# Opening of a two-layer attention and MLP kernel: resident bias, reordered row maxima, transposes moved to TensorE, held weight loads

## The chip, the cores and the metric

The kernel runs on one core of a Trainium2 chip. The metric is the device time of one execution in microseconds (us). The core's engines run their own instruction streams in order: TensorE (PE; its weight loads are listed apart as PEld), VectorE (DVE), ScalarE (ACT), GpSimd (POOL) and SyncE (SP), which here only issues transfers. ACT issues transfers too, on a queue of its own. An engine waits for another by semaphores.

## The reference

Two layers, each of windowed attention and a squared-ReLU MLP, over 2048 rows of width 640, in float32. Attention has 32 heads of width 20; each row sees itself and the 255 rows before it.

```python
def _A_ref(x, wqkv, wo):
    H = 32; Dh = D // H; W = 256
    qkv = (x @ wqkv).reshape(B, S, 3, H, Dh) ...
    scores = jnp.einsum("bhqd,bhkd->bhqk", q, k) * (Dh ** -0.5)
    mask = (idx[:, None] - idx[None, :] >= 0) & (idx[:, None] - idx[None, :] < W)
    p = _softmax(jnp.where(mask, scores, -1e9), axis=-1)
    return einsum("bhqk,bhkd->bhqd", p, v) ... @ wo

def _B_ref(x, w1, b1, w2, b2):
    h = jnp.maximum(x @ w1 + b1, 0)
    return (h * h) @ w2 + b2

x = x + _A_ref(_layernorm(x), wqkv, wo)
x = x + _B_ref(_layernorm(x), w1, b1, w2, b2)     # both lines twice
```

## The kernel before

**Units.** The rows of a layer are cut into 8 units of 256 rows; with two layers there are 16 units, u = 0 to 15. Every dense product is made of float16 pieces: an operand is split into a high and a low half, and three matmuls (high·high, high·low, low·high) per 128-deep slice are summed by `mm3` (L334), whose matmuls all carry L339. A matmul has 256 or 320 columns. Its accumulators, and the outputs of transposes (`tr`) and of p·v (`pv`), take turns in two PSUM tiles (`mm_tile`, L240, bufs=2): the third one waits until the first has been evicted. Evicting is mostly a pair: ACT writes the high half, then DVE the low half (L534 and L537 for queries and keys, L389 and L390 for transposed rows).

**Stages of a unit.** Layernorm (DVE, with one power on POOL); transposed rows `yT`; queries and keys (`stage_qk`), which are written to device memory, read back in another layout by head ("spread", L589) into `qt` and `kt`; values (`stage_v`); then 8 quads of 4 heads. A quad runs twice through the scores: first for the row maxima (`max_quad`: TensorE writes two PSUM blocks `bb`, DVE reduces them), then, with the maxima folded into the operands (`max_out` L783, a small transfer `qt<-mT` of L757), for the exponentials (`exp_quad`: TensorE, ACT L825, masks on POOL and DVE) and p·v (`pv_quad`, L931). Both passes use the same `bb`, so a pass waits until the engine that reads the one before it is done. After the last quad the unit's outputs, written to device memory (L951), come back (`load_o`, L969: transfers L984, L985), are divided by the row sums (L1017, L1020), split into halves (L1024, L1027) and multiplied by `wo` (`stage_o`), normalised, transposed by TensorE (`stage_y` for the opening, L403) or by transfers (`y_cross`), and go through the MLP (`stage_f`, with weights `w_s` and the intermediate `hh`).

**Order.** All five queues are written in an order that the program decides while it is built. Operations are posted as jobs with an engine, a cost, dependencies and a priority (`post`, L144); `pump` (L161) puts the jobs that can start by the planner's clock, and that clock decides how many dense matmuls go between two quads. `urgency` (L332, and L1381 from u = 1 on) holds priorities. In the opening (`ahead_all`, L1350, and `flow`, L1301) the quads of unit 0 are mixed with the dense work of units 0, 1 and 2; unit 0 has no rows before it, so its quads are smaller (L735, L886). The rows of unit 1 and 2 are transposed by transfers there (`ln_early`, L467, in which ACT L452 and DVE L456 make the two halves and SP transposes them, L459).

**Weights.** They are loaded in float32 and converted by ACT (L271) and DVE (L272) while the opening runs; `bulk` (L153) posts the loads of `wo`, `w1` and `w2` on ACT's queue when the planner takes the transfers to be idle. b2 is loaded and broadcast to all partitions in every unit (`add_b2`, L1066), into one of the two `xt` buffers that layernorm uses too; POOL adds it to the residual.

**An eviction's dependency.** In `evict` (L540), `left[k]` holds which unit last used the staging buffer, and the transfers that have read it. The comparison at L543 sets a tuple of two against a tuple of one, so it is always unequal, and every chunk is planned after the transfer of the chunk before it.

Of the kernel before, what the change touches and what calls it, by code (L numbers as in the profile page):

```python
# [10 lines left out]
F32 = mybir.dt.float32  # L11
# [5 lines left out]
P = 128  # L17
# [28 lines left out]
def kernel(ctx: ExitStack, tc: tile.TileContext, x, wqkv, wo, w1, b1, w2, b2, out):  # L46
# [35 lines left out]
    for h in range(2):  # L82
        nc.gpsimd.tensor_copy(drop[h * Q:(h + 1) * Q], edges[h * Q:(h + 1) * Q, :, h * Q:(h + 1) * Q])
    b1s = sb.tile([P, FC], F32, name="b1s")
    kts = []
    for i in range(3):
# [31 lines left out]
    TAIL = {"A": 115.0, "D": 85.0, "G": 40.0, "S": 0.0}  # L118

    class Job:  # L120
        def __init__(self, eng, cost, fn, deps, nb, prio, size=0, idle=False, land=LAND):
# [4 lines left out]
        def ready(self):  # L126
            return all(d.end is not None for d in self.deps)

        def start(self):
            t = max([clk[self.eng], self.nb] + [d.end + LAT for d in self.deps])  # L130
            return max(t, moved[0] - 2200.0) if self.idle else t

# [198 lines left out]

    urgency = {"out": 0, "od": 1, "cross": 1, "mask": 0, "turn": 1, "exp": 1, "ln": 1, "y": 0.5, "clear": 0.5}  # L332

# [168 lines left out]
    def stage_qk(u, which=(0, 1)):  # L502
# [9 lines left out]
        for j, c0 in order:  # L512
# [27 lines left out]
            def evict(wait, k=k, n=n, c0=c0, high=high, low=low, jobs=jobs, j=j, dst=dst, qd=qd):  # L540
                pr = urgency["out"]
                old = left.get(k, ())
                if k and (j, u) != old[:1]:  # L543
                    old = left[k] = ((j, u), [], old[1] if old else [])
                hi_ = post("A", 60 + 212 * n, high, *(old[2] if k else ()), wait=wait, prio=pr)
                lo_ = post("D", 70 + 267 * n, low, hi_, prio=pr)
                jobs.append(lo_)
                if u == 0:
                    wrote = leave(u, j, dst, qd, lo_, c0, n)
                elif c0 + n == KC:  # L550
                    wrote = leave(u, j, dst, qd, lo_, 0, KC)
                else:
                    return
                if k:
                    old[1].append(wrote)
# [17 lines left out]
    def leave(u, j, dst, qd, ready, c0, n):  # L573
# [17 lines left out]

        wrote = dma(write, n * P * 3 * T * 2, ready, n=2, prio=0)

# [15 lines left out]
    def stage_v(u, which=range(4)):  # L609
        yT = yTs[u]  # L610
        for i in range(2):
            if u == 2:
                yield Want(sums[i], bank=False)
            vt = vts[(2 * u + i) % 6][0]
            for h in range(2):
# [51 lines left out]
    def max_quad(n, later=False):  # L667
# [62 lines left out]
        else:  # L730
# [7 lines left out]
            apart[0] = True  # L738
            for w in range(4):
                j, i = divmod(w, 2)  # L740
                for e in range(2):
                    to = bb[e][:, w % 3, w // 3 * T:w // 3 * T + (1 + i) * P]
                    if i:
                        reduce(e, w, to, maskw, 2 * P)
                    else:
                        reduce(e, w, to, maskw[:, P:], P)
            mxjobs[u, G] = list(bbjobs)

# [220 lines left out]
    def load_o(u, late=False, free_=()):  # L969
# [16 lines left out]

        loaded = dma(load, P * (KC + 1) * T * 4, *wrote, *free_, n=2, prio=0)
        if u == NU - 1:
            both = sb.tile([P, 2, D], F32, name="x1", tag="qt", bufs=2)
            x1 = [both[:, i] for i in range(2)]  # L990
        elif u == NU - 2:

            x1 = [krow[(u - 1) % 3][:, i * D:(i + 1) * D] for i in range(2)]
        else:
            x1 = [sb.tile([P, D], F32, name="x1", bufs=2) for i in range(2)]
# [70 lines left out]
    def add_b2(u):  # L1066

        b2s = sb.tile([P, D], F32, name="xt", tag="xt", bufs=2)
        load = dma(lambda: nc.sync.dma_start(b2s, bass.AP(tensor=b2.tensor, offset=b2.offset, ap=[[0, P], [1, D]])),
                   P * D * 4)  # L1070
        js = []
        for i in range(2):
            for h in range(2):
                hs = slice(h * HD, (h + 1) * HD)
                js.append(post("G", 827, lambda x1=x1s[u, i], hs=hs:
                               nc.gpsimd.tensor_tensor(x1[:, hs], x1[:, hs], b2s[:, hs], op=ALU.add), load, prio=2))
        return js
# [223 lines left out]
    def flow(todo, dense):  # L1301
# [3 lines left out]
        while todo:  # L1305
# [15 lines left out]
            if kind == "m":  # L1321
                max_quad(n)
            elif kind == "r":
                max_out(u, G)
            elif kind == "s":
                quad = exp_quad(n)
            else:
                pv_quad(n, quad)
            pump()
# [20 lines left out]
    def ahead_all():  # L1350
        yield from stage_qk(0)
        ln_early(1, place)
        yield from stage_v(0, range(2))
        ln_load(2)
        yield from stage_v(0, range(2, 4))
# [12 lines left out]
    load_o(0)  # L1368
    dma(lambda: nc.sync.dma_start(b1s, b1.rearrange("(c p) -> p c", p=P)), 8192, *ols[0][2], prio=2)

    while not all(j.end is not None and j.end <= now[0] + LOOK for j in bbjobs):
        c = next(rest)
        if not isinstance(c, Want):
            used[0] += c
            step(c)
    left_over = 3 * (QKC + VC) - used[0]
    rate[0] = 320.0
    for u in range(1, NU):
        last = u == NU - 1
        if u == 1:  # L1380
            urgency.update({"out": 0, "od": 1.5, "cross": 1, "mask": 0, "turn": 0.7, "exp": 0.7, "ln": 0.5, "y": 1, "clear": 0.5})  # L1381
# [47 lines left out]
```

## Time and profile before

| | |
|---|---|
| time, median of 3 (lowest, highest) | 1560.52 us (1558.01, 1563.2) |
| the profiled execution: time, span | 1561.46 us, 1559.6 us |
| mean granted TensorE clock | 0.997 of full speed |
| PE idle in the whole span | 26.1 us |
| transfers | 162.16 MB, mean 104 GB/s |

The span runs from the first to the last instruction; 1.9 us lie around it. In rows of the timeline the first number is the start in us, the second the duration; then engine, line, operation, what it writes and reads, count, and in brackets the idle time before it and what ended it. [...]

### The profile page before, as it was taken

The page shows a single profiled execution, that of the slowest core. Times are in us where ns is not written, and L with a number is a line of the kernel's source. Part 1 is how long each engine was busy: PE and PEld are TensorE (multiplying, and loading weights), DVE is VectorE, ACT ScalarE, POOL GpSimd, SP SyncE. Part 2 cuts the span into 40 slices and gives each one's busy share as a digit, 9 for nine tenths or more (in the row PEclk, how much of TensorE's full clock was granted, in tenths as well). Part 3 has the DMA queues.
Part 4 walks back from the last instruction along what each step waited for, and adds up shares of the span by engine and source line. Part 5 has one row for each costly group of instructions (what it writes and reads, how often), then busy time and mean ns, then how long its engine had stood idle before and what let it go on. Part 6 is the DMA issues. An engine that isn't in the chain of part 4 may idle for free. (4 is left out here: it accounts for less than half of the span.)

```text
span 1559.6 us, 58897 instructions
## 1 busy us (share of the span) xinstructions
PE 1533.5 (98%) x25822; PEld 1198.6 (77%) x25822; DVE 1043.3 (67%) x2244; ACT 669.7 (43%) x1365; POOL 451.8 (29%) x847
## 2 busy tenths in 40 slices
PE   8998999999999999999999999999999999999999
PEld 6666778787787877878777787877878777786777
DVE  8878775666757667675666757667675676667642
ACT  4565435334453443435343453444435335354422
POOL 1223314232141331413224141321413214142412
PEclk9999999999999999999999999999999999999999
DMA  9975354352534424344462434425243342542120
GB/s 271 209 201 127 80 121 92 106 114 54 123 88 114 105 74 126 69 126 89 99 130 63 119 91 119 100 70 132 67 126 89 94 117 65 122 90 59 30 68 18
DMA packets 248745, 162.16 MB, mean 104 GB/s; under 512 B 96552, under 2 KB 232232, under 8 KB 248488
## 3 DMA queue, kind: packets, MB, share of 16 engines
q1 hardware_dynamic: 242120, 148.89, 38.7%
q10 hardware_dynamic: 6368, 9.50, 2.1%
q8 instruction: 202, 3.31, 0.9%
q14 instruction: 55, 0.45, 0.1%
HBM read 84.68 MB, written 52.95 MB: 88 GB/s over the span
## 5 line engine op out<-in xcount | busy, mean ns | idle before, releaser
L825 ACT ACTIVATE pt<-bb 128x640 f32<-128x640 f32 (+2 forms) x512 | 311.9, 684 | 167.6 <-PE bb L840 148.9
L854 POOL TENSOR_SCALAR_AFFINE_SELECT pt<-pt 64x256 f32<-64x256 f32 x448 | 199.3, 445 | 582.1 <-ACT pt L825 560.0
L339 PE MATMUL acc<-y,w_s 128*128 128x256 f16 x2880 | 330.2, 274 | 1.2 <-DVE y L390 1.2
L339 PE MATMUL acc<-w_s,hh 128*128 128x320 f16 (+1 forms) x2340 | 326.7, 297 | 0.1
L339 PEld LDWEIGHTS <-w_s 128*128 128x128 f16 x2880 | 276.4, 98 | 40.9 <-issue 2.0
L339 PEld LDWEIGHTS <-hh 128*128 128x128 f16 x2340 | 222.1, 98 | 86.8 <-issue 0.4
L720 DVE TENSOR_REDUCE mx<-bb 128x4 f32<-128x1024 f32 x224 | 273.2, 1224 | 6.8
L339 PE MATMUL acc<-yT,wq_s 128*128 128x256 f16 x2250 | 259.1, 273 | 3.0 <-DVE qd L537 1.2
L339 PEld LDWEIGHTS <-wq_s 128*128 128x128 f16 x2400 | 229.6, 98 | 37.3 <-issue 4.3
L863 DVE COPY_PREDICATED_SCALAR pt<-drop,zero 128x256 f32 x224 | 99.9, 497 | 134.3 <-ACT pt L825 133.8
L1130 DVE TENSOR_TENSOR hh<-r,hh 128x256 f16<-128x256 f32 x192 | 98.3, 525 | 110.8 <-ACT hh L1127 105.7
L931 PE MATMUL pv<-pt,vt 64*32 64x192 f32 (+5 forms) x3840 | 166.7, 302 | 0.9 <-DVE y L390 0.6
L943 ACT COPY ot<-pv 128x256 f32<-128x256 f32 x128 | 47.6, 372 | 276.1 <-PE bb L931 247.2
L1124 POOL TENSOR_TENSOR r<-r 128x256 f32<-128x256 f32 x192 | 121.9, 655 | 127.9 <-ACT r L1120 125.3
L931 PE MATMUL bb<-pt,vt 64*32 64x128 f32 (+3 forms) x3584 | 153.5, 301 | 0.0
L717 DVE COPY_PREDICATED bb<-maskq,bb 128x256 f32<-128x256 uint16 x224 | 93.8, 423 | 85.7 <-PE bb L703 80.0
L931 PEld LDWEIGHTS pv<-pt,vt 64*32 64x32 f32 (+1 forms) x3840 | 125.5, 106 | 31.7 <-issue 3.7
L339 PE MATMUL acc<-wo_s,od 128*128 128x320 f16 x960 | 139.6, 299 | 2.2 <-ACT od L1024 2.0
L339 PE MATMUL acc<-wq_s,yT 128*128 128x320 f16 x900 | 132.1, 302 | 5.0 <-DVE qd L537 4.2
L1120 ACT ACTIVATE r<-acc,b1s 128x256 f32<-128x256 f32 x192 | 81.1, 476 | 98.6 <-PE acc L339 96.5
L339 PEld LDWEIGHTS <-od 128*128 128x128 f16 x960 | 90.9, 98 | 40.6 <-ACT od L1024 2.3
L339 PEld LDWEIGHTS <-yT 128*128 128x128 f16 x900 | 87.1, 98 | 40.0 <-issue 6.2
(103 smaller groups left out, 1476.3 us busy)
## 6 DMA issues: line engine op xcount, KB each, us to landing
qt<-qk SPq DMA_DIRECT2D x30, 480.0 KB
kt<-qk SPq DMA_DIRECT2D x30, 480.0 KB
o<-ot SPq DMA_DIRECT2D x256, 42.0 KB
qk<-qd SPq DMA_DIRECT2D x15, 640.0 KB
od<-o SPq DMA_DIRECT2D x14, 640.0 KB
qk<-yl SPq DMA_DIRECT2D x13, 640.0 KB
xt<-in_A_x_dram SPq DMA_DIRECT2D x16, 320.0 KB
x<-in_A_x_dram SPq DMA_DIRECT2D x16, 320.0 KB
```

Of the source, the lines that this page charges most:

```text
L339: nc.tensor.matmul(acc, lhs(a, c), rhs(b, c), start=(k == 0), stop=(k == 3 * nk - 1))
L717: nc.vector.copy_predicated(wins[:, :, 4 * Q:], later, wins[:, :, :Q])
L720: nc.vector.tensor_reduce(most, wins[:, :, Q:], axis=mybir.AxisListType.X, op=ALU.max)
L825: return lambda: nc.scalar.activation(room_of(box)[:, a:b], bank[:, a:b], AF.Exp, scale=SCALE / (QS * QS))
L854: nc.gpsimd.affine_select(out=m, in_=m, pattern=[[0, 4], [-1 if k else 1, Q]], base=0, fill=0.0, compare_op=ALU.is_gt if k else ALU.is_ge, ...
L863: nc.vector.copy_predicated(m, drop[:, k:k + 1, :].bitcast(mybir.dt.uint16).to_broadcast([P, 4, Q]), zero.unsqueeze(1).to_broadcast([P, 4, ...
L931: nc.tensor.matmul(pv[h][32 * jj:32 * (jj + 1), q0 * Q:(q0 + w) * Q], vf[r, c:c + 32], boxes[e]["pt"][r, a:b], start=(k == 0), stop=(k == ...
L943: nc.scalar.copy(ot[:, qd % 2], to)
L1120: nc.scalar.activation(box["r"], acc[:, f, :], AF.Relu, bias=b1s[:, f0 + f:f0 + f + 1], scale=1.0 / (YS * WS))
L1124: nc.gpsimd.tensor_tensor(box["r"], box["r"], box["r"], op=ALU.mult)
L1130: nc.vector.tensor_sub(hh[:, 1, f, :], box["r"], hh[:, 0, f, :])
```

## The change

- b2 is loaded once into a tile of its own, `b2s`, after unit 0's output has been requested; the additions on POOL wait for no load of their own any more.
- `max_quad` for the first unit of a layer (units 0 and 8) posts the four reductions of one `bb` block, then the four of the other; for unit 8 the second four may be posted after the p·v of the quad beside it.
- In the opening, unit 1's rows are transposed by TensorE (`ln_t`), after the first half of unit 0's values; unit 2's remain with transfers.
- Bulk loads are held from the last p·v of unit 0 until the read of unit 0's output has been issued, by a marker job in `quiet`; a write of unit 2's queries or keys that is posted in that time waits too.
- The comparison in `evict` is made between like things, priorities of the opening change, and the later priorities set in from unit 3 instead of unit 1.

```diff
+    b2s = sb.tile([P, D], F32, name="b2s")
...
+    quiet = []
...
         def ready(self):
-            return all(d.end is not None for d in self.deps)
+            return all(d.end is not None for d in self.deps) and not (self.idle and any(q.end is None for q in quiet))
...
-            return max(t, moved[0] - 2200.0) if self.idle else t
+            return max([t, moved[0] - 2200.0] + [q.end for q in quiet]) if self.idle else t
...
-    urgency = {"out": 0, "od": 1, "cross": 1, "mask": 0, "turn": 1, "exp": 1, "ln": 1, "y": 0.5, "clear": 0.5}
+    urgency = {"out": 0, "od": 0.5, "cross": 1, "mask": 0, "turn": 1, "exp": 1, "ln": 1, "y": 1, "clear": 0}
...
-                if k and (j, u) != old[:1]:
+                if k and (not old or old[0] != (j, u)):
...
-        wrote = dma(write, n * P * 3 * T * 2, ready, n=2, prio=0)
+        wrote = dma(write, n * P * 3 * T * 2, ready, *(quiet if u == 2 else ()), n=2, prio=0)
...
                 yield Want(sums[i], bank=False)
+                need(sums[i])
...
-            for w in range(4):
-                j, i = divmod(w, 2)
-                for e in range(2):
-                    to = bb[e][:, w % 3, w // 3 * T:w // 3 * T + (1 + i) * P]
...
+            def each(e):
+                for w in range(4):
+                    i = w % 2
+                    reduce(e, w, bb[e][:, w % 3, w // 3 * T:w // 3 * T + (1 + i) * P], maskw[:, (1 - i) * P:], (1 + i) * P)
+                mxjobs[u, G] = list(bbjobs)
+
+            each(0)
+            behind.append(lambda: each(1))
+            if not later:
+                tops()
...
         loaded = dma(load, P * (KC + 1) * T * 4, *wrote, *free_, n=2, prio=0)
+        if u == 0:
+            loaded.gates.append(quiet[0])
...
-        b2s = sb.tile([P, D], F32, name="xt", tag="xt", bufs=2)
-        load = dma(lambda: nc.sync.dma_start(b2s, bass.AP(tensor=b2.tensor, offset=b2.offset, ap=[[0, P], [1, D]])),
-                   P * D * 4)
...
-                               nc.gpsimd.tensor_tensor(x1[:, hs], x1[:, hs], b2s[:, hs], op=ALU.add), load, prio=2))
+                               nc.gpsimd.tensor_tensor(x1[:, hs], x1[:, hs], b2s[:, hs], op=ALU.add), *b2load, prio=2))
...
+                if n == NQ - 1:
+                    quiet.append(Job("S", 0.0, None, [], 0.0, 0))
                 pv_quad(n, quad)
...
         yield from stage_qk(0)
-        ln_early(1, place)
         yield from stage_v(0, range(2))
+        yield from ln_t(1, place)
         ln_load(2)
...
-    left_over = 3 * (QKC + VC) - used[0]
+    left_over = 3 * (QKC + VC) + LNC - used[0]
...
-        if u == 1:
+        if u == 3:
             urgency.update({"out": 0, "od": 1.5, "cross": 1, "mask": 0, "turn": 0.7, "exp": 0.7, "ln": 0.5, "y": 1, "clear": 0.5})
```

The change moves instructions in all queues of the opening. From the end of unit 1's MLP on, the stream of TensorE is the same as before, instruction for instruction. Three places show what moved.

On ACT, at the end of unit 0's queries and keys (`qd` is the staging of queries, `stg` that of keys and, where an `xt` is read, of unit 1's rows; `vt` are values), before:

```order
L271 ACTIVATE wq_s<-kt_96 128x5x128 x3
L534 ACTIVATE qd<-acc 128x2x256
L534 ACTIVATE stg<-acc 128x2x256
L452 CAST stg<-xt 128x640
L300 DMA w_s<-in_A_wo_dram 32x5x640
L452 CAST stg<-xt 128x640
L534 ACTIVATE qd<-acc 128x256
L534 ACTIVATE stg<-acc 128x256
```

The same place of the changed kernel:

```order
L537 ACTIVATE qd<-acc 128x2x256
L274 ACTIVATE wq_s<-kt_97 128x5x128 x3
L537 ACTIVATE stg<-acc 128x2x256
L537 ACTIVATE qd<-acc 128x256
L537 ACTIVATE stg<-acc 128x256
L626 ACTIVATE vt_98<-acc 128x16x20
L303 DMA w_s<-in_A_wo_dram 32x5x640
L626 ACTIVATE vt_98<-acc 128x16x20
L392 CAST kt_97<-tr 128x3x128
L392 CAST kt_97<-tr 128x2x128
```

The last chunk's two evictions now stand right behind the chunk before; the two casts of unit 1's rows are gone, and the evictions of TensorE's transposes (`tr`) follow the values.

On SP, around the read of unit 0's output (`o`; `rs` and `od` are what is read, `qk_1` unit 2's keys, `mT` the maxima), before:

```order
L757 DMA qt<-mT 1x8x128 x4
L951 DMA o_720<-ot 21x2x256 x4
L984 DMA rs<-o_720 128x1x256
L985 DMA od<-o_720 128x5x256
L583 DMA qk_1_1596<-qd 128x5x512
L585 DMA qk_1_1596<-qd 128x5x256
L589 DMA qt<-qk_0_1344 60x16x256 x2
```

And in the changed kernel:

```order
L762 DMA qt<-mT 1x8x128 x4
L586 DMA qk_1_1543<-qd 128x5x512
L588 DMA qk_1_1543<-qd 128x5x256
L956 DMA o_763<-ot 21x2x256 x4
L989 DMA rs<-o_763 128x1x256
L990 DMA od<-o_763 128x5x256
L592 DMA qt<-qk_0_1297 60x16x256 x2
```

The write of unit 2's keys has moved from behind the read to ahead of the last write of `o`.

On DVE, where that output is divided and split (`mx` are maxima, `ot` the sum of two p·v halves, L863 and L868 clear masked weights), before:

```order
L946 TENSOR_TENSOR ot<-bb_143,ot 128x256
L1017 RECIPROCAL rs<-rs 128x64
L1020 TENSOR_TENSOR od<-od,rs 128x5x64
L1017 RECIPROCAL rs<-rs 128x64
L794 TENSOR_SCALAR mT<-tr 16x128
L795 SCALAR_TENSOR_TENSOR mT<-tr,mT 16x128
L1027 TENSOR_TENSOR od<-od 128x5x64
```

And in the changed kernel:

```order
L951 TENSOR_TENSOR ot<-bb_144,ot 128x256
L275 SCALAR_TENSOR_TENSOR w_s<-kt_97,w_s 128x640
L799 TENSOR_SCALAR mT<-tr 16x128
L800 SCALAR_TENSOR_TENSOR mT<-tr,mT 16x128
L1024 RECIPROCAL rs<-rs 128x64 x2
L1027 TENSOR_TENSOR od<-od,rs 128x5x64 x2
L868 COPY_PREDICATED pt<-drop,zero 128x4x64 x2
L1034 TENSOR_TENSOR od<-od 128x5x64 x2
```

The division now stands behind the maxima's rows `mT`, and so behind the second scores pass of unit 1.

More of the change, by code (lines that the diff above doesn't have):

```diff
@@ L738, in max_quad @@
             apart[0] = True
-            for w in range(4):
-                j, i = divmod(w, 2)
-                for e in range(2):
-                    to = bb[e][:, w % 3, w // 3 * T:w // 3 * T + (1 + i) * P]
[L743 to L747, printed above, removed]
+            def each(e):
[7 more added lines that the diff above has]
+                tops()
     mxjobs = {}
@@ L1369 @@
     dma(lambda: nc.sync.dma_start(b1s, b1.rearrange("(c p) -> p c", p=P)), 8192, *ols[0][2], prio=2)
+    b2load = [dma(lambda: nc.sync.dma_start(b2s, bass.AP(tensor=b2.tensor, offset=b2.offset, ap=[[0, P], [1, D]])),
+                  P * D * 4, *ols[0][2], prio=2)]
     while not all(j.end is not None and j.end <= now[0] + LOOK for j in bbjobs):
```

## The prediction

> **What bounds the kernel now.** First the page's head: one engine is busy nearly throughout.
>
> ```profile
> span 1559.6 us, 58897 instructions
> PE 1533.5 (98%) x25822; PEld 1198.6 (77%) x25822; DVE 1043.3 (67%) x2244; ACT 669.7 (43%) x1365; POOL 451.8 (29%) x847
> ```
>
> TensorE is idle for 26.1 us. Next, stretches of 10 us (PE, PEld, DVE, ACT and POOL busy with counts, granted clock, DMA share, GB/s), and stretches of 3.4 us around the two places where the clock falls.
>
> ```profile
> 20.00:30.00 10.00, 8.35 (x76) 7.18 (x74) 9.68 (x19) 3.94 (x7) 1.61 (x2) 1.00 0.83 206
> 30.00:40.00 10.00, 6.94 (x47) 4.09 (x47) 6.20 (x29) 1.72 (x4) 0.41 (x1) 0.83 1.02 211
> 160.00:170.00 10.00, 10.00 (x208) 8.48 (x206) 8.80 (x17) 6.36 (x15) 4.80 (x9) 1.00 0.52 102
> ...
> 30.83:34.24 3.41, 1.18 (x13) 0.67 (x13) 2.21 (x6) 1.28 (x3) 0.00 (x0) 1.00 0.98 172
> 34.25:37.65 3.40, 3.40 (x14) 1.96 (x13) 2.62 (x16) 0.44 (x1) 0.00 (x0) 0.50 0.92 220
> 126.41:129.81 3.40, 2.11 (x16) 1.38 (x14) 3.18 (x7) 0.78 (x2) 0.00 (x0) 1.00 0.44 122
> 136.65:140.05 3.40, 1.36 (x64) 1.16 (x64) 3.33 (x9) 1.73 (x4) 0.55 (x1) 1.00 0.53 184
> 140.06:143.46 3.40, 2.86 (x44) 2.20 (x45) 2.72 (x6) 1.55 (x4) 0.00 (x0) 0.50 0.00 0
> 143.47:146.88 3.41, 3.41 (x17) 2.43 (x16) 3.07 (x6) 2.49 (x4) 1.95 (x1) 0.50 0.16 22
> ```
>
> From 160 us on nothing is to be had; the opening holds the waits. After a stretch with 1.18 or 1.36 us busy of 3.4 the clock is halved for one or two stretches; after 2.11 it is not. TensorE's own waits, from its timeline:
>
> ```profile
> 25.45 3.44 PE L339 MATMUL acc<-yT,wq_s 128*128 128x256 f16 x30 [0.53 <-DVE qd L537]
> 33.06 0.70 PE L339 MATMUL acc<-wq_s,yT 128*128 128x320 f16 x4 [4.18 <-DVE qd L537]
> 47.61 0.27 PE L886 MATMUL bb<-qt,kt 62*128 62x256 f16 x1 [0.36 <-DMA qt<-mT]
> 48.14 0.49 PE L886 MATMUL bb<-qt,kt 62*128 62x256 f16 x7 [0.26 <-DVE bmv L370]
> ...
> 140.24 1.30 PE L403 MATMUL tr<-ident,xt 128*128 128x128 f32 x5 [1.78 <-DVE xt L378]
> 143.53 8.68 PE L339 MATMUL acc<-y,w_s 128*128 128x256 f16 x63
> ```
>
> The largest, 4.18 us, waits for a PSUM tile that DVE empties late.
>
> **Term 1, the late eviction.** ACT's and DVE's timelines:
>
> ```profile
> 27.60 0.73 ACT L452 CAST stg<-xt 128x640 f16<-128x640 f32 x1 [2.05 <-DVE xt L378]
> 31.09 0.72 ACT L452 CAST stg<-xt 128x640 f16<-128x640 f32 x1 [2.76 <-DVE xt L378]
> 31.72 0.38 ACT L534 ACTIVATE qd<-acc 128x256 f16<-128x256 f32 x1
> 32.59 0.42 DVE L537 SCALAR_TENSOR_TENSOR qd<-acc,qd 128x256 f16<-128x256 f32 x1
> ```
>
> The last query chunk's eviction at 31.72 stands behind a cast that waits for unit 1's layernorm. In the new order no cast is there, and the chunk before is evicted ahead of three weight conversions, which also covers the 0.53. Both waits go (4.7 us), and with them the 3.4 us at half clock from 34.25 (1.7). What is late next is the last chunk's DVE half, due by my reading of the queues 0.8 us ahead of TensorE's need. **-6.4 us**; bounds -7 and 0 (DVE, at 9.68 of 10 busy, late again).
>
> **Term 2, ten transposes on TensorE.** The group of ten near the end, and the eviction and reduction rows:
>
> ```profile
> L403 PE MATMUL bb<-ident,xt 128*128 128x128 f32 x10 | 1.4, 273 | 0.0
> L390 DVE TENSOR_TENSOR yT<-bb,yT 128x384 f16<-128x384 f32 (+1 forms) x4 | 1.9, 489 | 1.1 <-ACT yT L389 1.1
> ...
> 34.23 0.30 DVE L683 CUSTOM_DVE_ANT_0 bb<-bb,maskw 128x128 f32<-128x128 f32 x1 [0.90 <-PE bb L735]
> 36.72 0.14 DVE L683 DVE_READ_ACCUMULATOR2_ANT mx<- 128x1 f32 x1
> ```
>
> The transposes cost 1.4 us. Four groups (3, 2, 3, 2) take turns in two PSUM tiles, so the third waits for the first's eviction, and DVE has unit 0's first eight reductions (34.23 to 36.86, 2.6 us) around the four evictions (1.9): 4.6 us with the start, against 0.95 (seven matmuls of 0.136), 1.4 and 0.44 (a scores pass) on TensorE. That leaves **+1.8 us** of wait; bounds 0 and 3.5. The removed casts and transfers of unit 1 ran on engines that TensorE no longer waits for, so they give nothing beyond Term 1; SP gets free earlier.
>
> [...]
>
> **Term 3, first exponentials.** 25 more matmuls (2.7 us) stand between the maxima's transfer and the pass that waited 0.36 and 0.26: **-0.6**; bounds -0.6 and +1.
>
> **Term 4, the rest of unit 0's quads.** The waits view of 40 to 130 us:
>
> ```profile
> PE acc L339 <- DVE qd L537: 0.6, 1, 0.6
> PE acc L339 <- DVE stg L537: 0.6, 1, 0.6
> ```
>
> The new order spaces the quads nearly as before. One of these waits follows a maxima transpose that now has 25 matmuls instead of 5 behind it; I take half: **-0.6**; bounds -1.2 and +1.2. The reordered reductions are the same eight, and one pass reads both blocks alternately, so whichever is last counts: nothing.
>
> **Term 5, from the last p·v of unit 0 to the MLP of unit 0.** The pace of its pieces, from starts in TensorE's timeline:
>
> ```profile
> 104.05 4.54 PE L339 MATMUL acc<-yT,wq_s 128*128 128x256 f16 x40
> 108.52 0.76 PE L840 MATMUL bb<-qt,kt 62*64 62x128 f16 x38
> ...
> 162.89 0.76 PE L703 MATMUL bb<-kt,qt 60*64 60x256 f16 x38
> 164.88 2.90 PE L339 MATMUL acc<-y,w_s 128*128 128x256 f16 x25
> ...
> 1513.75 1.79 PE L339 MATMUL acc<-w_s,hh 128*128 128x320 f16 x12
> 1515.38 0.71 PE L403 MATMUL bb<-ident,xt 128*128 128x128 f32 x5
> ```
>
> A matmul takes 0.112 us (4.47 by 40) or, with 320 columns, 0.136 (1.63 by 12); a maxima pass and its p·v 2.0 (1.99), of which I give the pass 0.7. Unit 0's last p·v ended at 104.05, the MLP's first matmul ran at 143.53: 39.5 us. The stretch held 40 and 120 such matmuls, 7 scores passes, 3 p·v and 12 transposes: 31.1 us of work, 8.4 of waiting and half clock. Now the 40, 4 of the 120, one scores pass and a transpose lie outside it, which leaves 25.2 us. The chain beside them:
>
> ```profile
> 104.60 2.64 SPq L951 DMA_DIRECT2D o<-ot  x4
> 110.26 0.59 SPq L984 DMA_DIRECT2D rs<-o  x1
> 109.38 2.49 ACT L825 ACTIVATE pt<-bb 128x640 f32<-128x640 f32 x4 [0.27 <-issue]
> 113.50 0.42 DVE L717 COPY_PREDICATED bb<-maskq,bb 128x256 f32<-128x256 uint16 x1
> 116.70 0.41 DVE L946 TENSOR_TENSOR ot<-bb,ot 128x256 f32<-128x256 f32 x1
> 121.23 0.49 DVE L1027 TENSOR_TENSOR od<-od 128x320 f16<-128x320 f32 x1 [0.22 <-ACT od L1024]
> ```
>
> Counted from the end of that p·v: 30 matmuls, scores, 23 matmuls, maxima and p·v end at 10.5. Three matmuls are left, but the next scores need both reductions and the sum (113.50 to 117.11, 3.6 us): they start at 12.7, a wait of 1.8. The maxima pass directly behind needs four exponentials (2.5 us): 16.2, a wait of 2.6. The division, now behind `mT`, starts at 14.4, and its first half with masks and splits ends at 18.0 (before 17.7). P·v takes until 18.6, 30 matmuls with `wo` until 22.7. DVE has the second half of the division and split (3.0), the reductions and the sum (3.6) behind 18.0, so the next scores wait until 24.6 (1.9); then 30 matmuls, maxima and p·v end at 31.9. The second tile's transposes wait 1.7 for its layernorm, the MLP 1.4 for their eviction: it starts at 36.4, 11.2 us above its work. Against 8.4: **+2.8 us**; bounds -2 and +5. Holding the bulk loads frees the queue for the write and read of `o` (104.60 to 110.26 before), but the write of unit 2's keys now stands ahead of it, so I count no gain; the chain has cover until 14.4.
>
> **Term 6, the clock there.** Before, 3.4 us at half clock follow 143.53 (1.7 lost). Now 3.1 of some 3.7 us before the MLP are idle, so a fall is as likely as not: 1.4 expected, **-0.3**; bounds -1.7 and +1.7.
>
> **Costed at nothing.** 16 broadcasts of b2 become one, beside a DMA share of 0.52. POOL's four additions of a unit now run together, ahead of the squares:
>
> ```profile
> L1076 POOL TENSOR_TENSOR x<-x,xt 128x320 f32<-128x320 f32 x60 | 56.7, 956 | 92.5 <-DMA xt<-in_B_b_dram 81.1 <-issue 11.3
> ```
>
> 3.8 us, against 3.3 us of matmuls before the first square is due; uncovered, 0.5 a unit, 7.5 in all. Unit 8's deferred reductions lie beside a saturated TensorE; uncovered, a wait of 1.3 us per quad.
>
> **Sum.** -6.4 + 1.4 + 1.8 - 0.6 - 0.6 + 2.8 - 0.3 = -1.9 us. The profiled execution took 1561.46 (its span and 1.9 around it), so 1559.6 in its terms; it lies 0.9 above the median of 1560.52, so **1558.6 us**.
>
> **Rivals.** A difference under 0.3% (4.7 us) can hardly be told from none. (a) **The new waits don't show**: the transposes' evictions fit beside other work, the chain after the last p·v waits as long as before, the clock holds at the MLP. For it: before, these places waited mostly 0.3 to 1.8 us. Against it: dense work does run out there. -6.4 + 1.4 - 0.6 - 0.6 - 1.7 = -7.9, taken from 1560.5: 1552.6. (b) **The clock falls in more places**, ending slower: two half-clock stretches behind the transposes (+3.4), one that the waits of Term 5 don't hide (+1.7), two at the MLP instead of the half chance of one (+2.0): +7.1 on the forecast, 1565.7. It decides where a 3.4 us stretch is idle by more than about 1.3 to 2 us (above); Term 2's wait is just there. [...] (c) **The eviction stays late**, since DVE's conversions and not the cast held it: Term 1 goes, 6.4 on the forecast, 1565.0. Against it: ACT waited 2.76 us for that cast.
>
> **Chances.** Forecast 0.50, (a) 0.33, (b) 0.10, (c) 0.07. Faster by over 0.3%: (a) and a tail of the forecast, 0.36. Slower: (b) and the upper part of (c), 0.13. Within: 0.51. The forecast alone spans 1555 to 1562; leaving out 1 in 10 on each side, the range is 1551.5 to 1565.5.
>
> **What would show it.** Right: the values of unit 0 start near 28 us without a wait and at full clock; TensorE waits 1 to 3 us around the transposes near 33 to 36 us; from unit 0's last p·v to the MLP take 35 to 38 us, with waits at the scores behind three matmuls and the maxima behind them. The half clock appears once near the MLP, or not at all. From 160 us on TensorE stays full, and the two kernels differ by a constant. Wrong: waits for POOL in later units, a half clock near 35 us, or a division of `od` that waits for its transfer.

## The result and the profile after

The changed kernel takes **1569.95 us** (median of 6 runs, 1568.83 to 1571.78), the kernel before 1560.65 beside it (6 runs, 1558.01 to 1563.2): ratio 1.006, 95% interval 1.0048 to 1.0073, 9.3 us slower. Forecast were 1558.6 us and a range up to 1565.5; the time lies outside. The profiled execution took 1570.76 us. The page's head, after:

```profile
span 1569.0 us, 58829 instructions
PE 1537.4 (98%) x25832; PEld 1200.7 (77%) x25832; DVE 1044.9 (67%) x2246; ACT 670.8 (43%) x1367; POOL 444.3 (28%) x847
```

TensorE is idle for 31.6 us, before 26.1, and busy for 3.9 us more. The span is cut below at six points that both kernels have: the first matmul of unit 0's values, its first pass for exponentials, the end of its last p·v, its MLP's first matmul, a dense piece near 270 us and one near 1010 us. Three stretches of before, then five of after (length; busy time of PE, PEld, DVE, ACT and POOL; granted clock; DMA share; GB/s):

```profile
33.06:47.61 14.55, 14.07 (x106) 9.09 (x105) 10.93 (x58) 1.75 (x4) 0.55 (x1) 0.88 0.81 186
47.61:104.05 56.44, 54.21 (x650) 38.78 (x651) 41.68 (x129) 34.53 (x72) 14.60 (x33) 1.00 0.87 218
104.05:143.53 39.48, 34.64 (x634) 25.16 (x632) 35.77 (x71) 20.90 (x41) 7.35 (x14) 0.96 0.63 164
```

```profile
10.60:27.87 17.27, 16.56 (x151) 14.61 (x152) 16.92 (x29) 11.66 (x20) 0.55 (x1) 1.00 0.98 305
27.87:48.33 20.46, 18.32 (x143) 12.72 (x140) 16.83 (x68) 4.22 (x10) 1.09 (x2) 0.92 0.85 211
48.33:109.52 61.19, 55.39 (x671) 40.33 (x670) 49.09 (x141) 36.56 (x76) 15.88 (x33) 1.00 0.75 195
109.52:146.31 36.79, 28.60 (x552) 20.30 (x548) 29.99 (x58) 17.74 (x35) 10.09 (x18) 0.95 0.63 158
146.31:274.58 128.27, 127.64 (x2316) 100.59 (x2316) 86.24 (x170) 59.23 (x120) 38.03 (x74) 0.99 0.38 91
```

The values start 5.2 us earlier (27.87), as forecast, but the last p·v ends 5.5 us later (109.52). The first stretch has lost its waits; in the next three TensorE is idle for 2.1, 5.8 and 8.2 us, before for 0.5, 2.2 and 4.8.

Stretches hold different work in the two kernels, so a length alone misleads. **Loss** is here the length minus the work, and work is the count of pieces by their undisturbed pace between starts: 0.109 us a matmul of 256 columns, 0.1365 with 320, 0.69 and 0.44 a large and a small pass, 1.30 and 0.79 a large and a small p·v, 0.11 a transpose. In the traces 148 matmuls of 256 columns take 16.17 us from 11.70 (after), 91 of 320 take 12.36 from 1499.83 (after), the passes 0.69 from 154.00 (after) and 0.44 from 42.01 (before), the p·v 1.29 from 160.28 and 0.79 from 52.56 (after), five transposes 0.54 from 1522.52 (after). Example: 109.52 to 146.31 is 36.8 us, its pieces make 25.1, the loss is 11.7. Loss holds waits and half clock. A starts at the first dense matmul (10.84 us before, 10.68 after), G ends with the last one; G's 72 matmuls of 160 columns are counted like those of 320, which takes the same 4.9 us off G's loss in every column. All kernels of this table were profiled once; the work is that of before in the first and e2_red, that of after in the others.

| stretch | work before / after | before | after | e1_alt | e2_red | g2_half | g4_alt_steady1 | h1_alt_steady2 |
|---|---|---|---|---|---|---|---|---|
| A, to unit 0's values | 16.4 / 16.4 | 5.9 | 0.8 | 0.8 | 5.9 | 0.8 | 0.8 | 0.8 |
| B, to the first exponentials | 11.8 / 15.6 | 2.8 | 4.8 | 2.7 | 4.8 | 3.6 | 2.7 | 2.7 |
| C, to the last p·v | 48.9 / 51.1 | 7.5 | 10.1 | 6.8 | 10.0 | 8.0 | 8.2 | 7.0 |
| D, to the MLP | 30.8 / 25.1 | 8.7 | 11.7 | 11.6 | 7.9 | 14.4 | 14.0 | 12.2 |
| E, to about 270 us | 120.5 / 121.3 | 4.3 | 6.9 | 8.5 | 2.4 | 6.9 | 2.7 | 7.9 |
| F, to about 1010 us | 726.5 / 726.5 | 15.2 | 16.8 | 15.0 | 19.1 | 15.5 | 14.6 | 15.0 |
| G, to the end | 533.3 / 533.3 | 13.2 | 14.7 | 14.5 | 13.2 | 12.3 | 12.9 | 14.1 |

After against before, from values not yet rounded: -5.0 +2.1 +2.6 +3.0 +2.6 +1.6 +1.5 = 8.4 of loss and 1.1 of work, 9.5; the spans differ by 9.4, the rest lies ahead of A and behind G. How far one profile can be trusted shows in G: TensorE has the same instructions there in all 16 kernels, and the loss is 11.9 to 14.9 us, so a difference of 1 or 2 us between two single profiles says little by itself. TensorE's waits after, in 27 to 48, 48 to 110 and 109.5 to 146.4 us (in total, times, longest):

```profile
PE tr L406 <- DVE kt L393: 1.4, 1, 1.4
PE acc L342 <- DVE kt L393: 0.5, 1, 0.5
...
PE bb L891 <- DVE mx L687: 2.8, 3, 1.1
PE acc L342 <- DVE stg L540: 0.9, 1, 0.9
PE tr L794 <- DVE stg L540: 0.8, 1, 0.8
...
PE bb L845 <- DVE ot L951: 2.7, 2, 1.7
PE bb L707 <- ACT pt L830: 2.3, 2, 1.9
PE tr L406 <- DVE xt L381: 2.2, 1, 2.2
PE acc L342 <- DVE y L393: 0.9, 1, 0.9
```

The first two (transposes' evictions) and the last four (chain in front of the MLP) are forecast waits. `bb <- DVE mx L687` is not: passes for exponentials wait for the row maxima. DVE's timeline in the first quad shows why; a `READ_ACCUMULATOR2` of 0.14 us stands behind each reduction, and the block changes at the third row:

```profile
38.26 0.43 DVE L687 CUSTOM_DVE_ANT_0 bb<-bb,maskw 128x256 f32<-128x256 f32 x1
38.61 0.14 DVE L687 DVE_READ_ACCUMULATOR2_ANT mx<- 128x1 f32 x1
38.61 0.33 DVE L687 CUSTOM_DVE_ANT_0 bb<-bb,maskw 128x128 f32<-128x128 f32 x1
38.86 0.14 DVE L687 DVE_READ_ACCUMULATOR2_ANT mx<- 128x1 f32 x1
39.03 0.43 DVE L687 CUSTOM_DVE_ANT_0 bb<-bb,maskw 128x256 f32<-128x256 f32 x1
```

On the other block the reduction starts together with the read before it (38.61). On the same block it starts after that read is done (38.86 + 0.14, then 39.03): 0.42 us from start to start behind 128 columns, where before shows 0.25 (34.45 to 34.70, from a block to the other). Before, the blocks alternated and each reduction started together with the read before it: 2.6 us for eight (34.23 to 36.86). After, six of seven steps stay on a block, and eight take 3.5 (36.96 to 40.44): 0.14 us a step.

### The profile page after: what moved, and what is told of

The parts are those of the page before. It is cut to its first block, busy times and chain, and to the rows that moved or that the text cites. A ratio compares the mean times of both kernels' runs of the same rounds, so it can differ in the third digit from the quotient of the medians.

```text
span 1569.0 us, 58829 instructions
## 1 busy us (share of the span) xinstructions
PE 1537.4 (98%) x25832; PEld 1200.7 (77%) x25832; DVE 1044.9 (67%) x2246; ACT 670.8 (43%) x1367; POOL 444.3 (28%) x847
## 4 chain that ended last, share of the span: by engine, by line
PE 47%; DVE 2%; ACT 1%; DMA 1%; issue 0%; SPq 0%; ACTq 0%; DVEq 0%
PE acc L342 38%; PE pv L936 4%; PE bb L707 2%; PE bb L845 2%; PE bb L936 1%; DMA ov<-o 0%; ACT pt L830 0%; DVE mx L724 0%; PE bb L891 0%; DVE bb L721 0%; DVE od L1034 0%; DVE bb L687 0%; PE bb L739 0%; SPq L956 0%; DVE pt L868 0%
## 5 line engine op out<-in xcount | busy, mean ns | idle before, releaser
L868 DVE COPY_PREDICATED_SCALAR pt<-drop,zero 128x256 f32 x224 | 99.8, 498 | 148.3 <-ACT pt L830 144.1
L1134 DVE TENSOR_TENSOR hh<-r,hh 128x256 f16<-128x256 f32 x192 | 89.9, 480 | 108.1 <-ACT hh L1131 102.8
L936 PE MATMUL bb<-pt,vt 64*32 64x64 f32 (+3 forms) x3584 | 155.9, 303 | 0.0
L936 PEld LDWEIGHTS bb<-pt,vt 64*32 64x32 f32 x3584 | 117.6, 106 | 0.7 <-DVE pt L868 0.3
```

What stands on the lines that cost most here:

```text
L868: nc.vector.copy_predicated(m, drop[:, k:k + 1, :].bitcast(mybir.dt.uint16).to_broadcast([P, 4, Q]), zero.unsqueeze(1).to_broadcast([P, 4, ...
L936: nc.tensor.matmul(pv[h][32 * jj:32 * (jj + 1), q0 * Q:(q0 + w) * Q], vf[r, c:c + 32], boxes[e]["pt"][r, a:b], start=(k == 0), stop=(k == ...
L1134: nc.vector.tensor_sub(hh[:, 1, f, :], box["r"], hh[:, 0, f, :])
```

## The experiments

Diffs are against the changed kernel except in e2_red and e4_left. Before was timed in each job: 1561.57 (e), 1561.16 (f), 1560.11 (g), 1560.38 us (h).

| run | median us | ratio to before, 95% interval |
|---|---|---|
| e1_alt | 1563.63 | 1.0017, 1.0008 to 1.0027 |
| e2_red | 1566.61 | 1.0036, 1.0021 to 1.005 |
| e3_dma | 1600.95 | 1.025, 1.0232 to 1.0269 |
| e4_left | 1578.23 | 1.0113, 1.009 to 1.0136 |
| f1_alt_urg | 1564.15 | 1.0019, 1.001 to 1.0028 |
| f2_alt_nohold | 1564.81 | 1.0023, 1.0013 to 1.0032 |
| f3_alt_b2 | 1563.36 | 1.0016, 1.0007 to 1.0025 |
| f4_alt_urg_nohold | 1564.31 | 1.0017, 1.0006 to 1.0028 |
| g1_alt0 | 1563.52 | 1.003, 1.0018 to 1.0041 |
| g2_half | 1566.38 | 1.004, 1.0027 to 1.0054 |
| g3_alt_old0 | 1565.43 | 1.0039, 1.0025 to 1.0053 |
| g4_alt_steady1 | 1560.98 | 1.0003, 0.9995 to 1.0012 |
| h1_alt_steady2 | 1563.04 | 1.0013, 1.0004 to 1.0022 |
| h2_alt_steady1_nohold | 1563.17 | 1.0012, 1.0003 to 1.0021 |

**e1_alt: the old order of the reductions, all else changed.**

```diff
-            def each(e):
-                for w in range(4):
...
+            for w in range(4):
+                j, i = divmod(w, 2)
+                for e in range(2):
+                    to = bb[e][:, w % 3, w // 3 * T:w // 3 * T + (1 + i) * P]
...
```

> The changed kernel with the reductions of units 0 and 8 in the old order, the two score blocks taking turns (nothing deferred). Theory R: reductions that follow each other on one block each wait for the one before, so a quad takes 3.5 us on VectorE instead of 2.6, and TensorE pays for that between the first exponential pass and the last p.v of unit 0 (10.1 us of waiting against 7.5 before) and at the border of units 7 and 8. R expects 3 to 6 us less than the changed kernel, 1564 to 1567 us, and 2.6 us for the eight reductions. Rival: the waits there come from the other order of conversions and priorities; then under 1.5 us less.

The ratio falls from 1.006 to 1.0017: the order costs some 6.3 us by the medians (6.7 by the ratios), the larger part of the loss. The waits for `mx` of L687 at the exponentials are gone; in 48 to 110 us the largest left are 1.1 us for `mT` and 0.8 for `stg`. These are e1_alt's in 27 to 48 us:

```profile
PE tr L406 <- DVE kt L393: 0.7, 1, 0.7
PE acc L342 <- DVE kt L393: 0.5, 1, 0.5
PE tr L793 <- DVE mx L687: 0.2, 1, 0.2
PE tr L406 <- ACT vt L626: 0.2, 1, 0.2
```

The evictions of the transposes come earlier too, since they stand among the reductions. And the clock holds. Two stretches of after, then two of e1_alt:

```profile
33.57:36.98 3.41, 1.47 (x16) 1.06 (x16) 2.92 (x13) 1.12 (x3) 0.00 (x0) 1.00 1.10 226
36.98:40.39 3.41, 3.41 (x15) 1.95 (x14) 3.21 (x17) 0.00 (x0) 0.00 (x0) 0.50 0.93 256
```

```profile
31.65:35.06 3.41, 2.48 (x18) 1.61 (x17) 3.36 (x18) 1.31 (x4) 0.00 (x0) 1.00 0.97 225
35.06:38.47 3.41, 2.91 (x27) 2.11 (x27) 3.03 (x17) 0.81 (x3) 0.00 (x0) 1.00 1.17 217
```

After a stretch with 1.47 us busy the clock is halved, after 2.48 it is not; 19 matmuls behind the transposes take 4.42 us after and 2.74 in e1_alt.

**e2_red: before, with the new order of the reductions alone** (the same diff the other way round, in before).

> The kernel before with the new order of the reductions alone; all other engines' instruction streams are those of before, only VectorE's differs. Theory R expects 3 to 6 us more than before, 1563.5 to 1566.5 us, with eight reductions taking 3.5 us. Rival: within 1.5 us of before.

5.0 us slower, with TensorE's stream as before; the loss in B, C and F grows by 2.0, 2.5 and 3.9 us. From both sides the same: the order is a cause by itself.

**g2_half: an order with three of seven steps on the same block, without deferral.**

```diff
...
+            for w in range(4):
+                j, i = divmod(w, 2)
+                for e in ((0, 1) if w % 2 == 0 else (1, 0)):
...
```

> The changed kernel with the old place of the reductions (no deferral), in an order of which 3 of 7 steps stay on the same block (first, second, second, first, first, second, second, first), where the old alternating order has 0 and the new one 6. If each step on the same block costs DVE some 0.14 us by a wait for the step before, unit 0's first eight take about 2.6 + 3 x 0.14 = 3.05 us from the first start to the last end (2.6 alternating, 3.5 in the new order), and the time lies between the two, ratio 1.003 to 1.004. Rival, it is the first block's early end or the deferral that costs, not the steps: eight take 2.6 and the ratio is 1.0017.

The first and the last row of the first quad, and the waits for the maxima in 48 to 110 us:

```profile
36.69 0.29 DVE L687 CUSTOM_DVE_ANT_0 bb<-bb,maskw 128x128 f32<-128x128 f32 x1
...
39.60 0.14 DVE L687 DVE_READ_ACCUMULATOR2_ANT mx<- 128x1 f32 x1
```

```profile
PE bb L890 <- DVE mx L687: 1.5, 2, 0.8
```

3.05 us from 36.69 to 39.74, the number expected, and half of the waits (1.5 against 2.8 and none); B and C lose 11.5 us, against 9.4 in e1_alt and 14.9 after. So the steps on one block are the cost, with no deferral. The time lies between the two as well (1.004), but a part of it is another wait, in D (2.8 us more than e1_alt).

**g1_alt0: the old order in unit 0, the new one with deferral in unit 8.**

```diff
+            if u == 0:
+                for w in range(4):
...
+            else:
+                def each(e):
...
```

> The changed kernel with the alternating reductions in unit 0 alone; unit 8 keeps the new order and the deferral of the second block. Theory R by segments (after against e1_alt: +2.2 us from its quads before the exponentials, +3.4 up to unit 0's last p.v, +1.8 between 270 and 1010 us, where the border of units 7 and 8 lies; 0.7 less before 270): unit 8 costs about 2 us, so ratio to before about 1.003 against e1_alt's 1.0017, and the extra waits are the scores passes near 760 us. Rival: the price is paid in unit 0 alone, by the half clock behind the transposes: ratio 1.0017 and no longer passes near 760.

In 745 to 845 us, the border of units 7 and 8, after has two waits that before and e1_alt don't show; g1_alt0 has the second:

```profile
PE bb L845 <- DVE ot L951: 1.1, 1, 1.1
PE acc L342 <- DVE qd L540: 1.0, 1, 1.0
```

So unit 8 pays 1.0 to 2.1 us, and unit 0 the rest, some 4 to 5. The timed ratio 1.003 agrees but its interval overlaps e1_alt's, so the size for unit 8 rests on the two waits. e2_red shows both as well (0.9 and 1.0).

**e3_dma: unit 1's rows by transfers again, all else changed.**

```diff
-        yield from stage_v(0, range(2))
-        yield from ln_t(1, place)
+        ln_early(1, place)
+        yield from stage_v(0, range(2))
```

> The changed kernel with unit 1's rows transposed by transfers again, at their old place. Theory T: the ten transposes cost 1.1 us of work, 1.9 us of wait at their evictions and 1.7 us by the clock that falls behind them; T expects 3 to 5 us less than the changed kernel, 1565 to 1567 us, and no half clock between 30 and 45 us. Rival: the casts and transfers for unit 1 return ahead of evictions and the wait near 28 us comes back; then no gain or a loss.

Far slower, the opposite of a gain. TensorE's timeline there (`kt` holds unit 1's transposed rows):

```profile
39.49 0.27 PE L342 MATMUL acc<-kt,wq_s 128*128 128x256 f16 x1 [1.66 <-issue]
...
41.34 7.49 PE L342 MATMUL acc<-kt,wq_s 128*128 128x256 f16 x55
52.83 1.23 PE L342 MATMUL acc<-kt,wq_s 128*128 128x256 f16 x5 [4.00 <-DVE qd L540]
```

Unit 1's first matmul waits, 55 of them take until 48.83, and the next five start only at 52.83, after 4.0 us of waiting for an eviction; between 40.6 and 58 us the mean granted clock is 0.71. B loses 9.4 us in this way, against 4.8 in the changed kernel. The larger part comes later: D loses 28.3 us, against 11.7. This is its largest wait there (110.7 to 170.6 us), for the maxima of unit 1:

```profile
PE bb L845 <- DVE mx L724: 11.3, 5, 5.0
```

What makes DVE so late there was not tried. In sum the transposes' 1.4 us of work are needed with the rest of the change, not a cost.

**e4_left: before, with the mended comparison alone.**

```diff
-                if k and (j, u) != old[:1]:
+                if k and (not old or old[0] != (j, u)):
```

> The kernel before with the mended comparison in the eviction alone. If the mended comparison is what removed the wait of 4.18 us and the half clock behind it, 4 to 6.5 us less than before, 1554 to 1556.5 us. Rival: the cast of unit 1's rows still stands ahead of the last evictions, and the wait stays, within 1.5 us of before.

A falls to 0.8 as in after, so the comparison alone removes Term 1's waits; yet the time is 1.1% above before. New waits between 27 and 220 us take more than was won:

```profile
PE bb L703 <- ACT pt L825: 5.1, 5, 2.3
PE acc L339 <- DVE qd L537: 2.5, 2, 1.8
PE bb L703 <- DMA kt<-qk: 2.0, 1, 2.0
```

Half clock from 39.8 to 43.2, from 138.7 to 149.0 and from 207.0 to 213.8 us comes with them, and E alone loses 16.1 us. Which of these is the first cause was not tried.

**What is left in e1_alt** is 2 us above before where a gain of 1.9 was forecast, and most of the difference lies in E (8.5 against 4.3). f1 to f4 take further parts back, on top of the old order of the reductions.

f1_alt_urg, the old priorities:

```diff
-    urgency = {"out": 0, "od": 0.5, "cross": 1, "mask": 0, "turn": 1, "exp": 1, "ln": 1, "y": 1, "clear": 0}
+    urgency = {"out": 0, "od": 1, "cross": 1, "mask": 0, "turn": 1, "exp": 1, "ln": 1, "y": 0.5, "clear": 0.5}
-        if u == 3:
+        if u == 1:
```

> The changed kernel with the alternating reductions and, further, the priorities of before (od 1, y 0.5, clear 0.5 up to unit 0, the steady set from unit 1 on). e1_alt lost 4.2 us more than before between the first MLP matmul (140.67) and the common point near 270 (8.54 us of waiting and half clock against 4.34). Theory U, the priorities cost this: the stretch falls to about 4.5 us, the time to about 4 us below e1_alt, ratio to before about 0.9985 (1559 where before is 1561.5). Theory H, the hold costs it: the stretch keeps about 8.5 and the ratio stays about 1.0015. Theory B, the four additions of b2 on POOL cost it: the same as H here.

f2_alt_nohold, no hold:

```diff
-            return all(d.end is not None for d in self.deps) and not (self.idle and any(q.end is None for q in quiet))
+            return all(d.end is not None for d in self.deps)
-        wrote = dma(write, n * P * 3 * T * 2, ready, *(quiet if u == 2 else ()), n=2, prio=0)
+        wrote = dma(write, n * P * 3 * T * 2, ready, n=2, prio=0)
```

> The changed kernel with the alternating reductions and without the hold (bulk loads may start before unit 0's o is read). Theory H: between the MLP's first matmul and about 270 us the waiting falls from 8.5 to about 4.5 us, ratio about 0.9985. Theories U and B: it keeps about 8.5 there; the wait before the MLP (11.6 us) may grow by 0 to 3 where the read of o stands behind bulk loads; ratio 1.001 to 1.003.

f3_alt_b2, b2 loaded in each unit:

```diff
+        b2s = sb.tile([P, D], F32, name="xt", tag="xt", bufs=2)
+        load = dma(lambda: nc.sync.dma_start(b2s, ...), P * D * 4)
...
```

> The changed kernel with the alternating reductions and with b2 loaded once a unit into a tile of x's pool as before, so that POOL's additions wait for that load. Theory B: the stretch behind the MLP falls from 8.5 to about 4.5 us, ratio about 0.9985. Theories U and H: within 1 us of e1_alt, ratio about 1.001 to 1.002; a resident b2 is worth nothing.

f4_alt_urg_nohold, f1 and f2 together:

> The changed kernel with alternating reductions, the old priorities and no hold: of the change are left the mended comparison, unit 1's rows on TensorE and the resident b2. If the loss behind the MLP comes from priorities or hold, or both together: waiting there 4 to 5 us, before the MLP 8 to 9 us, so 1561.5 - 4.4 (opening up to the last p.v, 16.16 before and 10.25 in e1_alt, with 1.5 more work) = about 1557, ratio 0.997. If it comes from the transposes (other work is used up before the MLP, and dense matmuls are short behind it): ratio 1.001 as e1_alt, waiting behind the MLP 8 us.

All four agree in time with e1_alt; none of the theories wins as stated. But the losses moved. D and E are 11.6 and 8.5 us in e1_alt, 16.2 and 4.1 in f1, 14.2 and 6.2 in f2, 11.3 and 7.5 in f3, 16.7 and 4.4 in f4. The old priorities take the losses behind the MLP away and have as much in front of it. What grows in front is for the most part half clock: in f1's D the same 551 matmuls are busy 3.4 us longer than in e1_alt's (32.05 against 28.61, granted clock 0.83 against 0.95), and TensorE is idle 1.2 us longer. So the priorities were taken apart.

g3_alt_old0 takes the first half of f1's diff, g4_alt_steady1 the second, h1_alt_steady2 the switch at unit 2; h2_alt_steady1_nohold is g4 with f2's diff.

> The changed kernel with the alternating reductions and the old priorities up to the switch (od 1, y 0.5, clear 0.5), the switch staying at unit 3. f1_alt_urg (both parts old) had 16.2 us of waiting before the MLP and 4.1 behind it, e1_alt 11.6 and 8.5. If the switch's place sets the small waits behind the MLP: 16 and 8 (slower, ratio 1.004). If the three numbers set both: as f1, ratio 1.002. If they set the wait before the MLP and the switch the ones behind it: the other half run gives 11.6 and 4.1 and is faster than before.

> The changed kernel with the alternating reductions, the new three priorities, and the switch to the steady set at unit 1 as before. If the two parts are separable (new numbers: short wait before the MLP; early switch: few waits behind it): 11.6 us before the MLP, 4.1 behind it, 1563.6 - 4.4 = about 1559, ratio 0.9985. If the steady set is what pushes od and the layernorm out before the MLP: 16 and 4, ratio 1.002.

> The changed kernel with the alternating reductions, the new three priorities, and the switch to the steady set at unit 2 (3 in the change, 1 before). The stretch from unit 0's last p.v to 270 us is unit 1's. If unit 1's part under the changed priorities makes the small waits behind the MLP: 11.6 us before the MLP and 7 to 8.5 behind it, as e1_alt, ratio 1.0017. If unit 2's part made them (work of unit 2 taken too early or too late): 11.6 before and 3 to 4 behind, ratio 0.999.

> g4_alt_steady1 without the hold: of the change are left the mended comparison, the transposes, the resident b2 and the three numbers in unit 0. If the hold shortens the way of o (write, read, layernorm) as f2_alt_nohold showed (14.2 us before the MLP against 11.6 with it): 16 to 17 before the MLP against 14.0, behind it 1 to 2.7, ratio 1.001. If it only moves waits from one side of the MLP to the other: ratio 1.0003 as g4.

With the switch at unit 1 E is 2.7 us (g4), with the switch at unit 2 7.9 (h1), at unit 3 8.5 (e1_alt) and, with the old three numbers, 9.4 (g3). So the place of the switch, and of it unit 1's part, makes the losses behind the MLP. This is not the accident of where a stretch at half clock lies: with half of the half-clock time taken off, E loses 2.4 to 2.8 us in all six profiles with the switch at unit 1 (before, e2_red, f1, f4, g4, h2) and 4.0 to 7.0 in all eight with a later one (e3_dma and e4_left, with their waits of another kind, left aside). In D g3 loses 12.2 us with the old three numbers, so these don't make the 16 of f1; h2 loses 16.6 in D and 3.0 in E. D and E of e1_alt, then of g4:

```profile
104.02:140.67 36.65, 28.61 (x551) 20.22 (x548) 29.89 (x58) 17.73 (x35) 10.09 (x18) 0.95 0.58 159
140.67:270.57 129.90, 128.40 (x2317) 100.69 (x2317) 86.20 (x170) 59.23 (x120) 38.05 (x74) 0.99 0.39 90
```

```profile
105.49:144.60 39.11, 31.05 (x551) 21.96 (x548) 31.64 (x60) 17.87 (x35) 10.28 (x18) 0.87 0.63 165
144.60:268.69 124.09, 123.92 (x2317) 99.16 (x2317) 85.31 (x168) 58.06 (x120) 39.04 (x75) 1.00 0.38 86
```

In D TensorE is idle for 8.0 us in e1_alt and 8.1 in g4; g4's D is longer by the clock: 0.87 in 39.1 us is three stretches of 3.4 us at half speed, 0.95 in 36.7 is one. One of the two more is the stretch that e1_alt has just behind the MLP's first matmul, in E. In E e1_alt is idle for 1.5 us, g4 for 0.2, and the same 2317 matmuls are busy for 4.5 us longer, 1.7 of it by that half clock. A part of the rest shows in the weight loads: p·v waits for masks (L867) and the product with `wo` for `od`. e1_alt, 144.5 to 270.6 us; g4 has none of these:

```profile
PEld pv L935 <- DVE pt L867: 0.5, 1, 0.5
PEld L342 <- DVE od L1033: 0.3, 1, 0.3
```

The remaining 2 us or so stay without a name. Of the 5.8 us that g4 wins in E, 2.5 go again in D and 1.4 in C. g4, with the comparison, the transposes, the hold, the resident b2 and the new three numbers in unit 0, is the fastest version tried: 1.0003 (0.9995 to 1.0012), the same as before, where 0.9985 was expected with D at 11.6. The hold shortens the waits of D: without it TensorE is idle there for 10.0 us in f2, 9.5 in h2 and 10.7 in f4, with it for 8.0 in e1_alt, 8.1 in g4 and 9.2 in f1. That it saves time isn't shown: the ratios are 1.0023 and 1.0017, 1.0012 and 1.0003, 1.0017 and 1.0019, with intervals that overlap. One edit, the added `need(sums[i])`, is in all these runs and was not taken back alone. Nothing tried beats before.

## Why the prediction was wrong, step by step

**Term 1, late eviction (-6.4): mechanism right.** A lost 5.0 us of waits in every kernel with the mended comparison. The other 1.7, the half clock behind, did not go in after: it moved to 36.98. In e1_alt, with the old order of the reductions, it is gone, as forecast.

**Term 2, transposes (+1.4 and +1.8): right in e1_alt, short in after.** The waits in B are 1.6 us in e1_alt (0.7, 0.5, 0.2, 0.2). After they are 2.1, with 1.7 of half clock: a piece of rival (b), at the place it named, but brought on by the reductions' order.

**Term 3 (-0.6)** is worth about -0.4: the first exponentials wait 0.22 in place of 0.36 and 0.26.

**Term 4 (-0.6) is the step that failed**, at "The reordered reductions are the same eight, and one pass reads both blocks alternately, so whichever is last counts: nothing." They are the same eight but not in the same time: 3.5 us instead of 2.6. With the old order C loses 0.8 us less than before, near the term's 0.6, but not by the waits that it names: TensorE is idle for 2.7 us there, before for 2.2, so that the number came out is partly luck. With the new order C loses 2.6 more. It also costs 2.1 in B, and 1.8 in F, where the deferral was held to be free. The trace shows for these reductions, with a read of 0.14 us behind each: a step to another reduction on the same tile costs 0.14 us more than one to the other tile (3.5 against 2.6 us, six such steps against none), with the number of operations unchanged.

**Term 5, in front of the MLP (+2.8): right in sum, +3.0, in part by luck.** The stretch is 36.8 us against 36.4 worked out, and all five waits named are there. After's timeline:

```profile
122.09 0.76 PE L845 MATMUL bb<-qt,kt 62*64 62x128 f16 x37 [1.66 <-DVE ot L951]
124.98 0.27 PE L707 MATMUL bb<-kt,qt 60*64 60x256 f16 x1 [1.92 <-ACT pt L830]
...
134.55 0.75 PE L845 MATMUL bb<-qt,kt 62*64 62x128 f16 x37 [1.08 <-DVE ot L951]
...
144.63 0.74 PE L406 MATMUL tr<-ident,xt 128*128 128x128 f32 x5 [2.21 <-DVE xt L381]
146.31 1.01 PE L342 MATMUL acc<-y,w_s 128*128 128x256 f16 x4 [0.94 <-DVE y L393]
```

Expected were 1.8, 2.6, 1.9, 1.7 and 1.4, 9.4 us; 7.8 came, and a stretch at half clock (125.73 to 129.14, 1.7 us) that the term did not have happens to make up for it.

**Term 6 (-0.3)** is 0: the clock falls at the MLP again (146.21 to 149.62).

**Behind 160 us "the two kernels differ by a constant": wrong.** E loses 2.6 us more than before (4.2 in e1_alt), because the opening's priorities now hold in unit 1 too (g4 against h1); the prediction gave that edit no term. G loses 1.5 more, by a fall of the clock in the last unit. The rows of after on both sides of it, and of before at the same work:

```profile
1446.68:1450.08 3.40, 1.44 (x43) 0.72 (x31) 2.04 (x6) 2.65 (x5) 1.11 (x3) 1.00 0.19 55
1450.08:1453.48 3.40, 3.32 (x81) 2.13 (x88) 2.83 (x6) 0.19 (x1) 1.34 (x3) 0.50 0.00 0
```

```profile
1437.11:1440.52 3.41, 2.16 (x49) 1.28 (x46) 2.33 (x6) 1.58 (x3) 0.16 (x1) 1.00 0.19 52
1440.52:1443.93 3.41, 2.62 (x103) 1.81 (x106) 2.62 (x8) 1.26 (x3) 2.29 (x5) 1.00 0.02 3
```

Both have the same wait of some 2 us. In before it is split between two stretches, after it lies in one. By these rows G's loss is where the stretches happen to lie, not a doing of the change. The other profiles agree: with the same TensorE instructions 7 of the 16 have a fall in G and 9 have none, and g4, which has most of the change, is among the nine.

**The account.** Forecast -1.9, measured +9.3: 11.2 us apart. The reductions' order makes 6.3 of them (after against e1_alt), E some 4 and G 1.3 (e1_alt against before); the three come to 11.8, and the 0.6 too much are not told apart from the small gains of the other terms and the spread of single profiles. **Rivals:** (a) and (c) are refuted, the new waits show and the eviction is early; of (b) one of the two stretches behind the transposes came true, and the one among the waits of Term 5, but no second one at the MLP, and (b) too put the reductions at nothing. b2 resident is worth nothing (f3), as costed.

## What to carry to other kernels

When operations of one engine are put in another order, compare the distance between their starts and not only their number: here eight reductions took 2.6 us in an order that alternates between two tiles, 3.5 tile by tile. Work brought forward into a place that waited isn't saved if a chain sets the length of the stretch it left; here 5.7 us of TensorE work went from D, and D became only 2.7 us shorter. A mended planning error can expose others: alone it cost 1.1%, and with the whole change except the transposes 2.5%.

## What the runs showed of the hardware

- From the start of a reduction, with its `READ_ACCUMULATOR2` of 0.14 us, to the start of the next: 0.38 to 0.43 us behind 128 columns and 0.53 to 0.56 behind 256 where the next is on the same PSUM tile, 0.20 to 0.25 and 0.35 to 0.38 where it is on the other (the first eight of before, after and g2_half).
- In after the clock is at half for stretches of 3.41 us on one raster: those from 36.98, 125.73 and 1450.10 us are 26 and 388 stretches of 3.4133 us apart, to within 0.05 us. In eight traces (before, after, g1_alt0, g2_half, g3_alt_old0, g4_alt_steady1, h1_alt_steady2, h2_alt_steady1_nohold), each cut on its own raster from 10 to 1545 us, the 15 stretches at full clock with TensorE busy for at most 1.4 us were all followed by half clock, of the seven with 1.45 to 1.75 five were, and of those with 1.9 or more none. After's stretch from 33.57 with 1.47 is one of the five, before's from 27.42 with 1.46 one of the two others. Before's stretch at half clock from 140.06, with 2.86 busy, was followed by a second.
